# Six weight pieces converted beside the attention instead of ten, a later pipeline for each piece, nine paired slices, and routing steps moved

## The chip, the cores and the metric

The kernel runs on one core of a Trainium2 chip. The metric is the device time of one execution in microseconds (us), as the median of several runs. On the core five engines work side by side, each through its own list of instructions in order: PE (TensorE, the matmuls; its weight loads are shown apart), DVE (VectorE), ACT (ScalarE), POOL (GpSimd) and SP (SyncE), which here issues the transfers of the DMA engines. The order on each engine is the order in which the program's lines run; an instruction that waits holds up all that stand behind it on its engine.

## What is computed

Three layers follow one another, for 4 sequences of 576 positions (2304 tokens) and a model width of 512.

```python
scores = scale * np.matmul(q, k.transpose(0, 1, 3, 2))        # 4 batches, 8 heads of 64
Dmat = np.where(rel >= 0, gamma ** rel, 0.0)                  # a decay for each head, no softmax
attn = np.matmul(scores * Dmat, v)
...
x = attn rearranged to (2304, 512)
h = ((x @ w_a) * (x @ w_b)) @ w_out                           # 512 -> 1536 -> 512
...
logits = h @ w_gate + modality_bias[modality_id]              # 8 experts
e_idx = np.argmax(logits, axis=1)
gate_w = softmax(logits)[e_idx]
out[mask] = gate_w * (np.maximum(h[mask] @ w1[e], 0) @ w2[e]) # for each expert e: 512 -> 1024 -> 512
```

The three weights of the middle layer (`w_a`, `w_b`, `w_out`) come as float64, read as pairs of 32-bit words, and are turned into float32 on the chip. Nearly all products are made from a high and a low part (`xh`, `xl`; `w[:, 0]`, `w[:, 1]`), three matmuls for each.

## The kernel before

**Attention.** A loop over `i` from -1 to 20 (L476) handles 20 chunks of up to 128 rows, five for each sequence (64, 128, 128, 128, 128 rows). In iteration `i` the program issues the loads of chunk i+4 on SP, scales chunk i+1 on POOL (`a_scale`), makes its scores on PE (`sc`, L358), multiplies the scores of chunk i by the mask on DVE (`rt`, L371), and lets PE make the output of chunk i from the carried state (`o`, L409), the new state (`S`, L390) and the output from `rt` (`o`, L422). Three chunks of 384 tokens stay on the core or are written to `xsp` and fetched again later (`a_spill`, L465; `load_x`, L1020; `split_x`, L1022 to L1025, a cast on ACT and a subtraction on POOL).

**Weight pieces.** The dense layer's weights are 12 slices `fc` of three pieces each (columns of `w_a`, columns of `w_b`, rows of `w_out`), 36 pieces in the order of use. The class `Conv` takes each piece through stages, one for each call of `cv.step`: a load of 512 KB by SP (L250), ACT's Abs (L259), four DVE operations (L262, L266, L270, L274), and at the end ACT's cast (L281) with a DVE subtraction (L282) behind it. `cv.step(new)` first advances the pieces that are under way and then loads `new` more. Ten pieces pass through it beside the attention, the rest in the hooks of the dense layer, as many for each step as `CV_MOE` says.

**Dense layer.** It has 72 steps, one for each chunk of 384 tokens and each slice. A step is `gemm1` (24 matmuls into two PSUM banks `ab`, L597; then `a` on ACT, `g` on DVE L605, `gh` on ACT, `gl` on DVE L609), the step's hooks, and then `gemm2` of the step before (9 matmuls into three banks `acc`, L617). The first two token chunks (n = 1 and 2) take the slices alternately up to slice `PAIR`, so that a weight slice is needed only every second step; after these, chunk 1 does the rest of its slices and then chunk 2 (steps up to 23). From step 24 on there are 12 steps for each of the other four chunks.

**Routing.** When a chunk has its last step, its three tiles of 128 tokens are routed in parts that `route_parts` makes: part 0 and part 1 are four dot products each on DVE (`scr`, L534), part 2 is the choice of the expert on DVE (ending in `ohb`, L556), part 3 two small matmuls on PE (`rk`, L565 and L566) and the token's place behind them. A table says in which of the following hooks each part (tile, part) stands: `halves` for the first chunk, `one_each` for the next, `spread` for the last one, whose parts fall into the first two slots of the expert layer. The entry 0 is put directly behind the chunk's last `gemm2`.

**Experts.** Slots of 384 tokens of one expert follow (`slot`, L918; matmuls L881 and L898), each with loads and splits of the next slot's weights and the gather of its tokens as hooks.

Of the kernel before, what the change touches and what calls it, by code (L numbers as in the profile page):

```python
# [99 lines left out]
def build(  # L100
# [17 lines left out]
    ctx.enter_context(  # L118
        tc.manual_schedule(engines={ET.PE, ET.DVE, ET.Activation, ET.SP, ET.Pool})
    )  # L120
    CV_ATT = 10
    CV_AT = (2, 3, 4, 6, 7, 8, 11, 12, 13, 16)
    SPILL = 0
    CV_MOE = (2, 1, 2, 1, 2, 2, 1, 2, 2, 2, 2, 1, 2, 2, 2, 0)
    PAIR = 8
    WARM = (6, 4)

    cp = ctx.enter_context(tc.tile_pool(name="cp", bufs=1))
# [24 lines left out]
    def unit(name, shape, dt=F32):  # L153
        return up.tile(shape, dt, name=name, tag="u")
# [74 lines left out]
    class Conv:  # L229
# [23 lines left out]
        def advance(self, c):  # L253
            c["n"] += 1
            i, raw = c["i"], c["raw"]
            fc, j = divmod(i, 3)
            if c["n"] == 2:
                t = c["t"] = unit(f"cv{i}", [P, 512], U32)
                nc.scalar.activation(out=t.bitcast(F32), in_=raw[:, :, 1].bitcast(F32), func=AF.Abs)  # L259
            elif c["n"] == 3:  # L260
                t = c["t"]
                nc.vector.tensor_scalar(  # L262
                    out=t.bitcast(F32), in0=t.bitcast(F32), scalar1=k1, scalar2=k2,
                    op0=ALU.max, op1=ALU.min,
                )
                nc.vector.tensor_scalar(  # L266
                    out=t, in0=t, scalar1=3, scalar2=0x3FFFFFFF,
                    op0=ALU.logical_shift_left, op1=ALU.bitwise_and,
                )
                nc.vector.scalar_tensor_tensor(  # L270
                    out=t, in0=raw[:, :, 0], scalar=29, in1=t,
                    op0=ALU.logical_shift_right, op1=ALU.bitwise_or,
                )
                nc.vector.scalar_tensor_tensor(  # L274
                    out=t, in0=raw[:, :, 1], scalar=0xC0000000, in1=t,
                    op0=ALU.bitwise_and, op1=ALU.bitwise_or,
                )
            elif c["n"] == 4:
                t = c["t"]
                w = wts[fc][j] = unit(f"w{fc}_{j}", [P, 2, 512], F32R)  # L280
                nc.scalar.copy(w[:, 0, :], t.bitcast(F32))  # L281
                nc.vector.tensor_sub(w[:, 1, :], t.bitcast(F32), w[:, 0, :].bitcast(F32))  # L282
                self.live.remove(c)
# [12 lines left out]
    chunks = [(b, c) for b in BATCHES for c in range(5)]  # L296
    n_ch = len(chunks)
# [131 lines left out]
    def a_spans(i):  # L429
        b, c, n, r0 = geo(i)  # L430
        t0 = r0
        while t0 < r0 + n:
            ch = t0 // NT
            m = min(r0 + n, (ch + 1) * NT) - t0
            yield ch, t0 - r0, t0 % NT, m
            t0 += m
# [9 lines left out]
    def a_lo(i):  # L446
        for ch, a, d, m in a_spans(i):
            if ch in ORDER[:2]:
                xh, xl = xt[ch]
                for hf in range(2):  # L450
                    k = slice(NP // 2 * hf, NP // 2 * (hf + 1))
                    nc.vector.tensor_sub(
                        xl[:, k, d : d + m], A[i]["o"][hf][:, :, a : a + m],
                        xh[:, k, d : d + m].bitcast(F32),
                    )
            elif d + m == NT:
                spill.append((i + SPILL, ch))
        A[i].clear() if chunks[i][1] == 4 else None
# [9 lines left out]
    cv = Conv()  # L468
# [7 lines left out]
    for i in range(-1, n_ch + 1):  # L476
        if 3 <= i + 4 < n_ch:
            a_load(i + 4)
        if i + 1 < len(WARM):
            warm(WARM[i + 1])  # L480


        if i == -1:
            a_turn(0)
            a_turn(1)
        if 0 <= i + 1 < n_ch:
            a_scale(i + 1)
            a_scores(i + 1)
        if 0 <= i < n_ch:
            a_mask(i)  # L490
        if i >= 1:
            a_lo(i - 1)
            a_spill(i - 1)
        if i >= 0 and chunks[min(i, n_ch - 1)][1] > 0:
            cv.step(1 if cv.loaded < CV_ATT and i in CV_AT else 0)
        if 1 <= i and i + 2 < n_ch:
            a_turn(i + 2)
        if 0 <= i < n_ch:
            a_inter(i)
            a_state(i)  # L500
            a_blocks(i + 1)
            a_intra(i)
            a_hi(i)
        if i == 0:
            a_turn(2)
# [516 lines left out]
    def split_x(at, k):  # L1022
# [2 lines left out]
        nc.gpsimd.tensor_sub(xl[:, k, :], xl[:, k, :].bitcast(F32), xh[:, k, :].bitcast(F32))  # L1025

    halves = {
        0: [(0, 0)],
        1: [(0, 1), (1, 0)],
        2: [(1, 1)],  # L1030
        3: [(2, 0), (2, 1)],
        5: [(0, 2)],
        6: [(0, 3), (1, 2)],
        8: [(1, 3), (2, 2)],
        10: [(2, 3)],
    }
    one_each = {i: [divmod(i, 4)] for i in range(12)}
    quick = {
# [14 lines left out]
        6: [(2, 0)],  # L1053
        8: [(1, 3), (2, 1)],
        9: [(2, 2)],
        10: [(2, 3)],
    }


    steps = [(n, fc) for fc in range(PAIR) for n in ORDER[:2]]  # L1060
    steps += [(n, fc) for n in ORDER[:2] for fc in range(PAIR, NFA)]
    steps += [(n, fc) for n in ORDER[2:] for fc in range(NFA)]
# [3 lines left out]
    for i in range(2 * NFA):  # L1066
        hooks[i].append(lambda i=i: cv.step(CV_MOE[min(i, len(CV_MOE) - 1)]))
    hooks[1].append(setup)
# [160 lines left out]
```

## Time and profile before

| | before |
|---|---|
| median of 3 runs | 781.68 us (781.29 to 782.35) |
| the profiled execution's own time | 781.75 us |
| its span, first to last instruction | 779.9 us |
| mean granted TensorE clock | 0.989 |
| busy share PE / weight loads / DVE / ACT / POOL | 97% / 88% / 61% / 34% / 20% |
| attention, first slice's `gemm1` of the dense layer begins at | 85.1 us |

All rows below are from the profiled execution; their times count from the start of its span, which lies 1.85 us (781.75 less 779.9) inside its own time. A busy PE is not a PE at its full rate, so busy shares tell where another engine was the limit only when they are read for a stretch.

### The profile page before, as it was taken

The numbers are of one execution on the slowest core, as the hardware profiler recorded it, in microseconds if no ns is written. First come the engines' busy times: TensorE is split into PE (matmuls) and PEld (weight loads), VectorE is DVE, ScalarE is ACT, GpSimd is POOL, SyncE is SP. The second block draws the span as 40 slices with busy tenths as digits, with TensorE's granted clock in tenths as the row PEclk, the third lists the DMA queues.
The fourth block names the chain that finished last, engine by engine and source line by source line (L and its number), as shares of the span: only waits on it lengthen the run. The fifth ranks groups of instructions, "written<-read, shape, count | busy, mean of one in ns | idle before, by whom it ended". The sixth has DMA issues, their size and how long they took to land.

```text
span 779.9 us, 12645 instructions
## 1 busy us (share of the span) xinstructions
PE 753.1 (97%) x4818; PEld 684.4 (88%) x4818; DVE 472.7 (61%) x1222; ACT 264.5 (34%) x519; POOL 154.1 (20%) x181
## 2 busy tenths in 40 slices
PE   7979999999899999999999999999999999999994
PEld 4867899998799899999999999999998899999993
DVE  1699658888768565444554456766887744445520
ACT  2546334444222211221122112125443525353611
POOL 6656000000011310110021000123215233140302
PEclk9999999999999999999999999999999999999998
DMA  9997702231412000200020001042845485465201
GB/s 298 346 373 285 274 9 101 82 108 54 136 54 82 1 1 1 82 1 0 1 82 1 1 0 41 1 146 113 315 161 81 158 286 173 128 199 176 82 1 46
DMA packets 29446, 87.31 MB, mean 112 GB/s; under 512 B 6591, under 2 KB 6751, under 8 KB 29376
## 3 DMA queue, kind: packets, MB, share of 16 engines
q1 hardware_dynamic: 25040, 76.49, 29.3%
q0 software_dynamic: 4336, 9.92, 4.1%
q8 instruction: 40, 0.66, 0.4%
q14 instruction: 30, 0.25, 0.1%
HBM read 73.64 MB, written 13.01 MB: 111 GB/s over the span
## 4 chain that ended last, share of the span: by engine, by line
PE 72%; DVE 15%; DMA 7%; issue 3%; ACT 2%; SPq 0%; POOLq 0%; DVEq 0%; ACTq 0%; POOL 0%
PE ab L597 30%; PE acc L617 15%; PE h L881 11%; PE y L898 10%; DMA idt<-perm,gidx 6%; DVE scr L534 3%; DVE cv L270 2%; DVE w L282 2%; DVE cv L266 2%; PE sc L358 1%; PE o L422 1%; DVE gl L609 1%; DVE g L605 1%; DVE cv L262 1%; ACT gh L607 1%
## 5 line engine op out<-in xcount | busy, mean ns | idle before, releaser
L597 PE MATMUL ab<-xh,w 128*128 128x384 f32 x1152 | 275.9, 336 | 2.9 <-ACT w L281 1.9
L597 PEld LDWEIGHTS ab<-xh,w 128*128 128x128 f32 x1152 | 208.7, 188 | 9.4 <-ACT w L281 2.2
L597 PE MATMUL ab<-xl,w 128*128 128x384 f32 x576 | 163.0, 337 | 0.0
L617 PE MATMUL acc<-w,gh 128*128 128x512 f32 x432 | 113.5, 398 | 0.0
L605 DVE TENSOR_TENSOR g<-ab,a 128x384 f32<-128x384 f32 x72 | 40.0, 556 | 120.1 <-ACT a L603 97.1
L534 DVE SCALAR_TENSOR_TENSOR scr<-row,wg 128x512 f32<-128x512 f32 x144 | 104.7, 729 | 4.6 <-ACT row L521 0.5
L597 PEld LDWEIGHTS ab<-xl,w 128*128 128x128 f32 x576 | 105.7, 188 | 1.0
L603 ACT COPY a<-ab 128x384 f32<-128x384 f32 x72 | 34.4, 478 | 187.8 <-PE ab L597 187.8
L617 PEld LDWEIGHTS acc<-w,gh 128*128 128x128 f32 x432 | 79.5, 189 | 12.7
L607 ACT CAST gh<-g 128x384 fp32r<-128x384 f32 x72 | 36.9, 513 | 114.5 <-DVE g L605 114.5
L815 DVE TENSOR_TENSOR el<-er,eh 128x1024 fp32r<-128x1024 f32 x56 | 67.8, 1222 | 12.5 <-ACT eh L814 12.5
L609 DVE TENSOR_TENSOR gl<-g,gh 128x384 fp32r<-128x384 f32 x72 | 40.2, 558 | 41.7 <-ACT gh L607 41.7
L888 DVE SCALAR_TENSOR_TENSOR hl<-h,hh 128x384 fp32r<-128x384 f32 x48 | 26.7, 555 | 63.8 <-ACT hh L886 59.0
L881 PE MATMUL h<-sh,el 128*128 128x384 f32 x192 | 64.7, 337 | 0.0
L881 PE MATMUL h<-sh,eh 128*128 128x384 f32 x192 | 64.7, 337 | 0.0
L881 PE MATMUL h<-sl,eh 128*128 128x384 f32 x192 | 64.5, 336 | 0.0
L617 PE MATMUL acc<-w,gl 128*128 128x512 f32 x216 | 61.3, 392 | 0.0
L1025 POOL TENSOR_TENSOR xl<-xl,xh 128x384 fp32r<-128x384 f32 x16 | 19.9, 1265 | 196.2 <-ACT xh L1024 177.3
L814 ACT CAST eh<-er 128x1024 fp32r<-128x1024 f32 x56 | 57.5, 1042 | 2.2 <-DMA er<-in_w1r_dram 2.2
L577 POOL DMA_INDIRECT perm<-tg,ix x18 | 18.8, 1046 | 195.8 <-DVE ix L575 170.3
L886 ACT ACTIVATE hh<-h 128x384 fp32r<-128x384 f32 x48 | 23.6, 492 | 95.9 <-PE h L881 87.2
L617 PEld LDWEIGHTS acc<-w,gl 128*128 128x128 f32 x216 | 40.6, 188 | 9.3
(165 smaller groups left out, 1003.0 us busy)
## 6 DMA issues: line engine op xcount, KB each, us to landing
er<-in_w1r_dram SPq DMA_DIRECT2D x28, 512.0 KB, 4.7
er<-in_w2r_dram SPq DMA_DIRECT2D x28, 512.0 KB, 5.0
raw<-in_wab_dram SPq DMA_DIRECT2D x24, 512.0 KB, 6.6
kv<-in_kv_dram SPq DMA_DIRECT2D x16, 512.0 KB, 8.2
raw<-in_wout_dram SPq DMA_DIRECT2D x12, 512.0 KB, 5.8
x2d<-row SPq DMA_DIRECT2D x18, 256.0 KB, 2.3
qk<-in_qf_dram SPq DMA_DIRECT2D x16, 256.0 KB, 8.1
xsp<-xf SPq DMA_DIRECT2D x4, 768.0 KB, 5.0
```

The lines of the kernel that those rows point to most:

```text
L534: nc.vector.scalar_tensor_tensor(out=scr, in0=row, scalar=1.0, in1=wg[e // 2][:, e % 2, :], op0=ALU.mult, op1=ALU.mult, accum_out=R["l"][: ...
L597: nc.tensor.matmul(ps[j], lhsT=ws[j][:, wi, k, :], rhs=x[:, k, :], start=(k == 0 and q == 0), stop=(k == KC - 1 and q == 2),)
L603: nc.scalar.copy(a, ps[0])
L605: nc.vector.tensor_mul(g, ps[1], a)
L607: nc.scalar.copy(gh, g)
L609: nc.vector.tensor_sub(gl, g, gh.bitcast(F32))
L617: nc.tensor.matmul(accs[t], lhsT=x[:, t * P : (t + 1) * P], rhs=w[:, wi, :], start=(fc == 0 and q == 0), stop=(fc == NFA - 1 and q == 2),)
L814: nc.scalar.copy(hi, raw)
L815: nc.vector.tensor_sub(lo, raw, hi.bitcast(F32))
L881: nc.tensor.matmul(ps, lhsT=w[:, fc % 2, k, :], rhs=x[:, k, :], start=(k == 0 and q == 0), stop=(k == KC - 1 and q == 2),)
L888: nc.vector.scalar_tensor_tensor(out=hl, in0=ps, scalar=0.0, in1=hh.bitcast(F32), op0=ALU.max, op1=ALU.subtract)
L898: nc.tensor.matmul(y, lhsT=x[:, t * P : (t + 1) * P], rhs=w, start=(fc == 0 and q == 0), stop=(fc == NFF - 1 and q == 2),)
```

## The change

In `Conv` each stage comes one call of `cv.step` later: the Abs in the third call instead of the second, the four DVE operations in the fourth, the cast and the subtraction in the fifth. `cv.step` stands before `a_lo` and `a_spill` in the attention loop, and it runs in every iteration from 1 on, where it had left out the first chunk of each sequence. The numbers of pieces loaded change: 12 loads stand in the attention, six of them so late that these pieces are still under way when the dense layer begins, and 24 in the dense layer instead of 26. `PAIR` is 9 instead of 8, so that chunk 1 has its last step at 20 instead of 19, and chunk 2 at 23 as before; the loads and `split_x` of the third chunk come one hook later with it. The table `halves` is written anew, and in `spread` the last tile's last part stands one hook later. The counts of instructions on the engines are the same; line numbers in the changed kernel are one or two lower.

```diff
-    CV_ATT = 10
-    CV_AT = (2, 3, 4, 6, 7, 8, 11, 12, 13, 16)
+    CV_ATT = {2: 1, 4: 1, 6: 1, 9: 1, 11: 1, 14: 1, 17: 2, 18: 1, 19: 2, 20: 1}
-    CV_MOE = (2, 1, 2, 1, 2, 2, 1, 2, 2, 2, 2, 1, 2, 2, 2, 0)
-    PAIR = 8
+    CV_MOE = (2, 2, 1, 2, 1, 2, 2, 1, 2, 1, 2, 2, 1, 2, 1, 0)
+    PAIR = 9
...
-            if c["n"] == 2:
+            if c["n"] == 3:
...
-            elif c["n"] == 3:
+            elif c["n"] == 4:
...
-            elif c["n"] == 4:
+            elif c["n"] == 5:
...
         if i >= 1:
+            cv.step(CV_ATT.get(i, 0))
             a_lo(i - 1)
             a_spill(i - 1)
-        if i >= 0 and chunks[min(i, n_ch - 1)][1] > 0:
-            cv.step(1 if cv.loaded < CV_ATT and i in CV_AT else 0)
...
     halves = {
-        0: [(0, 0)],
-        1: [(0, 1), (1, 0)],
-        2: [(1, 1)],
-        3: [(2, 0), (2, 1)],
-        5: [(0, 2)],
-        6: [(0, 3), (1, 2)],
-        8: [(1, 3), (2, 2)],
-        10: [(2, 3)],
+        0: [(0, 0), (0, 1)],
+        1: [(1, 0), (1, 1)],
+        2: [(2, 0), (2, 1)],
+        3: [(0, 2)],
+        4: [(0, 3), (1, 2)],
+        5: [(1, 3)],
+        6: [(2, 2)],
+        8: [(2, 3)],
     }
...
     spread = {
-        10: [(2, 3)],
+        11: [(2, 3)],
```

The first place is DVE in the attention, from the mask product of chunk 9 to that of chunk 11 (`rt9` to `rt11`; `cv3` and `w0_2` are pieces of weights). Before:

```order
L371 TENSOR_TENSOR rt9_691<-sc9_0_616,mask_89 128x512
L371 TENSOR_TENSOR rt9_691<-sc9_1_617,mask_89 128x512
L282 TENSOR_TENSOR w0_2_694<-cv2_570,w0_2_694 128x512
L262 TENSOR_SCALAR cv3_636<-cv3_636 128x512
L266 TENSOR_SCALAR cv3_636<-cv3_636 128x512
L270 SCALAR_TENSOR_TENSOR cv3_636<-raw3_505,cv3_636 128x512
L274 SCALAR_TENSOR_TENSOR cv3_636<-raw3_505,cv3_636 128x512
L371 TENSOR_TENSOR rt10_746<-sc10_0_681,mask_89 64x4x64
L371 TENSOR_TENSOR rt10_746<-sc10_1_682,mask_89 64x4x64
L371 TENSOR_TENSOR rt11_796<-sc11_0_736,mask_89 128x512
```

The same place on DVE in the changed kernel:

```order
L370 TENSOR_TENSOR rt9_674<-sc9_0_606,mask_89 128x512
L370 TENSOR_TENSOR rt9_674<-sc9_1_607,mask_89 128x512
L281 TENSOR_TENSOR w0_1_677<-cv1_561,w0_1_677 128x512
L370 TENSOR_TENSOR rt10_727<-sc10_0_664,mask_89 64x4x64
L370 TENSOR_TENSOR rt10_727<-sc10_1_665,mask_89 64x4x64
L261 TENSOR_SCALAR cv2_680<-cv2_680 128x512
L265 TENSOR_SCALAR cv2_680<-cv2_680 128x512
L269 SCALAR_TENSOR_TENSOR cv2_680<-raw2_501,cv2_680 128x512
L273 SCALAR_TENSOR_TENSOR cv2_680<-raw2_501,cv2_680 128x512
L370 TENSOR_TENSOR rt11_781<-sc11_0_717,mask_89 128x512
```

Before, a subtraction and the four operations of the next piece stood together between two mask products, and none in the next gap; now one of the two kinds stands in each gap, and the piece is one behind.

The second place is DVE after step 20 of the dense layer, where chunk 1 (tiles 3, 4 and 5) is routed while chunk 2 does its last slices (`g2_9` is chunk 2, slice 9; a row with x2 is two dot products). Before:

```order
L609 TENSOR_TENSOR gl2_8_2506<-g2_8_2502,gh2_8_2504 128x384
L534 SCALAR_TENSOR_TENSOR scr3_0_2527,l3_2526<-row3_2517,wg0_2411 128x512 x2
L534 SCALAR_TENSOR_TENSOR scr3_0_2527,l3_2526<-row3_2517,wg1_2413 128x512 x2
L605 TENSOR_TENSOR g2_9_2560<-ab2_9_1_2533,a2_9_2546 128x384
L609 TENSOR_TENSOR gl2_9_2564<-g2_9_2560,gh2_9_2562 128x384
L534 SCALAR_TENSOR_TENSOR scr3_4_2566,l3_2526<-row3_2517,wg2_2415 128x512 x2
L534 SCALAR_TENSOR_TENSOR scr3_4_2566,l3_2526<-row3_2517,wg3_2417 128x512 x2
L534 SCALAR_TENSOR_TENSOR scr4_0_2572,l4_2571<-row4_2520,wg0_2411 128x512 x2
L534 SCALAR_TENSOR_TENSOR scr4_0_2572,l4_2571<-row4_2520,wg1_2413 128x512 x2
L605 TENSOR_TENSOR g2_10_2618<-ab2_10_1_2591,a2_10_2604 128x384
```

DVE in the changed kernel, from the same chunk's last step (now slice 9 of chunk 2 stands ahead of the first dots):

```order
L607 TENSOR_TENSOR gl2_9_2549<-g2_9_2545,gh2_9_2547 128x384
L532 SCALAR_TENSOR_TENSOR scr3_0_2570,l3_2569<-row3_2560,wg0_2454 128x512 x2
L532 SCALAR_TENSOR_TENSOR scr3_0_2570,l3_2569<-row3_2560,wg1_2456 128x512 x2
L532 SCALAR_TENSOR_TENSOR scr3_4_2575,l3_2569<-row3_2560,wg2_2458 128x512 x2
L532 SCALAR_TENSOR_TENSOR scr3_4_2575,l3_2569<-row3_2560,wg3_2460 128x512 x2
L603 TENSOR_TENSOR g2_10_2608<-ab2_10_1_2581,a2_10_2594 128x384
L607 TENSOR_TENSOR gl2_10_2612<-g2_10_2608,gh2_10_2610 128x384
L532 SCALAR_TENSOR_TENSOR scr4_0_2615,l4_2614<-row4_2563,wg0_2454 128x512 x2
L532 SCALAR_TENSOR_TENSOR scr4_0_2615,l4_2614<-row4_2563,wg1_2456 128x512 x2
L532 SCALAR_TENSOR_TENSOR scr4_4_2620,l4_2614<-row4_2563,wg2_2458 128x512 x2
L532 SCALAR_TENSOR_TENSOR scr4_4_2620,l4_2614<-row4_2563,wg3_2460 128x512 x2
L603 TENSOR_TENSOR g2_11_2666<-ab2_11_1_2639,a2_11_2652 128x384
```

The 24 dots of the three tiles stood between the steps 20 to 24, as 4, 8, 4 and 8; now they start one step later and stand as 8, 8 and 8 in front of the same end. After them DVE has the choice for tile 3 behind step 24 (before: behind step 25), and the choice for tile 4 behind step 25 (before: 27).

The third place is PE, where the place of tile 4 is asked for (`rk4`). Before, it stood behind `gemm1` of step 28 (`ab0_4`) and ahead of `gemm2` of step 27:

```order
L597 MATMUL ab0_4_1_2975<-xh0_2471,w4_1_1670 128x384
L565 LDWEIGHTS tri_94
L565 MATMUL rk4_3018<-ohb4_2901,tri_94 128x8
L566 LDWEIGHTS ones_95
L566 MATMUL rk4_3018<-ohb4_2901,ones_95 128x8
L617 MATMUL acc0_0_2814<-w3_2_1552,gh0_3_2946 128x512
```

PE in the changed kernel at the same instruction:

```order
L595 MATMUL ab0_2_1_2856<-xh0_2514,w2_1_1361 128x384
L563 LDWEIGHTS tri_94
L563 MATMUL rk4_2907<-ohb4_2837,tri_94 128x8
L564 LDWEIGHTS ones_95
L564 MATMUL rk4_2907<-ohb4_2837,ones_95 128x8
L615 MATMUL acc0_0_2843<-w1_2_1224,gh0_1_2801 128x512
```

The two small matmuls stand behind `gemm1` of step 26 now (`ab0_2`), two steps earlier on PE, and `gemm2` of step 25 stands behind them.

## Rows read from the trace of the kernel before

**Rows 1.** The page, part 1: busy time, share of the span and instructions.

```profile
PE 753.1 (97%) x4818; PEld 684.4 (88%) x4818; DVE 472.7 (61%) x1222; ACT 264.5 (34%) x519; POOL 154.1 (20%) x181
```

**Rows 2.** Busy time in attention's second part: span, PE, PEld, DVE, ACT, POOL, clock, DMA.

```profile
34.80:85.10 50.30, 44.84 (x784) 36.96 (x781) 47.27 (x79) 28.33 (x67) 25.36 (x27) 0.97 0.90 322
```

**Rows 3.** Chain of waits, 20 to 86 us: start, length, engine and tile.

```profile
22.16 1.09 PE sc L358 x16
...
25.57 0.61 PE sc L358 x16
...
28.39 1.09 PE sc L358 x16
...
31.15 1.09 PE sc L358 x16
...
34.04 0.90 PE o L422 x16
```

**Rows 4.** Timeline of PE in the attention: start, length, instruction [idle before, releaser].

```profile
51.59 0.89 PE L422 MATMUL o<-rt,kv 64*64 64x64 f32 x16 [2.90 <-DVE rt L371]
```

**Rows 5.** Groups of DVE instructions, 34.8 to 85.1 us: busy us, mean ns, idle before.

```profile
L282 DVE TENSOR_TENSOR w<-cv,w 128x512 fp32r<-128x512 f32 x9 | 8.0, 894 | 2.0 <-ACT w L281 2.0
```

**Rows 6.** Chain of waits, 0 to 330 us, in the paired steps.

```profile
102.06 4.18 PE ab L597 x24
...
108.33 4.18 PE ab L597 x24
...
147.24 1.25 DVE w L282 x2
...
159.12 1.26 DVE w L282 x2
...
166.48 1.26 DVE w L282 x2
```

**Rows 7.** Timeline of PE in the paired steps and behind them.

```profile
133.23 0.33 PE L597 MATMUL ab<-xh,w 128*128 128x384 f32 x1
...
207.81 0.44 PE L597 MATMUL ab<-xh,w 128*128 128x384 f32 x1 [1.86 <-ACT w L281]
...
218.22 1.55 PE L617 MATMUL acc<-w,gh 128*128 128x512 f32 x6
```

**Rows 8.** Busy time behind that wait, columns as in rows 2.

```profile
208.00:212.00 4.00, 3.89 (x14) 3.47 (x14) 1.34 (x3) 0.65 (x2) 0.00 (x0) 0.64 0.84 267
```

**Rows 9.** Timeline of DVE while chunk 1 is routed.

```profile
220.66 0.69 DVE L534 SCALAR_TENSOR_TENSOR scr<-row,wg 128x512 f32<-128x512 f32 x1 [0.47 <-ACT row L521]
...
226.37 0.69 DVE L534 SCALAR_TENSOR_TENSOR scr<-row,wg 128x512 f32<-128x512 f32 x1
...
233.37 0.55 DVE L605 TENSOR_TENSOR g<-ab,a 128x384 f32<-128x384 f32 x1
...
239.17 0.55 DVE L605 TENSOR_TENSOR g<-ab,a 128x384 f32<-128x384 f32 x1
...
240.78 0.69 DVE L534 SCALAR_TENSOR_TENSOR scr<-row,wg 128x512 f32<-128x512 f32 x1
...
246.40 0.55 DVE L605 TENSOR_TENSOR g<-ab,a 128x384 f32<-128x384 f32 x1
...
259.22 0.16 DVE L541 TENSOR_TENSOR l<-l,mb 128x8 f32<-128x8 f32 x1
...
261.21 0.16 DVE L541 TENSOR_TENSOR l<-l,mb 128x8 f32<-128x8 f32 x1
```

**Rows 10.** Timeline of POOL in the same stretch.

```profile
226.35 3.00 POOL L1025 TENSOR_TENSOR xl<-xl,xh 128x384 fp32r<-128x384 f32 x2 [140.69 <-ACT xh L1024]
```

**Rows 11.** Timeline of PE, first place of chunk 1.

```profile
256.62 0.18 PE L565 MATMUL rk<-ohb,tri 128*128 128x8 bf16 x1 [0.64 <-DVE ohb L556]
```

**Rows 12.** Timelines of PE and of DVE, last chunk's routing in slot 1.

```profile
591.43 0.17 PE L565 MATMUL rk<-ohb,tri 128*128 128x8 bf16 x1 [1.62 <-DVE ohb L556]
...
598.31 0.17 DVE L832 CAST iid<-idt 128x3 uint32<-128x3 f32 x1 [3.67 <-DMA idt<-perm,gidx]
```

## The prediction

> **What bounds the kernel now.** The page comes first: PE is busy over 97% of the span [rows 1], so a gain can only lie in the few places where PE waits or runs slower than it could, and a loss wherever the change makes it wait anew. The second view is the busy time by stretch. From 34.8 us to the end of the attention PE has 44.84 us of 50.30, but DVE has 47.27 [rows 2]: there DVE is the fuller engine, by more than the whole span shows. The third view is the chain of waits, since it tells whether PE's own work would have ended earlier. Where it runs from PE to PE, the starts of the scores give the length of an iteration that only PE limits [rows 3]: 3.41 us (22.16 to 25.57), 2.82, 2.76, and a regular one of 3.79 (31.15 to 34.04, and .90 for the `o` that ends it). Behind that the chain leaves PE, and PE's timeline shows why: at 51.59 it had stood 2.90 us for a mask product `rt` on DVE [rows 4]. The fourth place is the paired steps. There a step of PE alone is 6.27 us (102.06 to 108.33) [rows 6], and later ones are longer. The fifth is the routing behind step 20, where DVE has little room between two steps [rows 9]. In the experts PE has few waits; one of 1.62 us is touched by the change [rows 12].
>
> **A. Attention.** I count what PE alone would take for iterations 7 to 19: five regular ones at 3.79, two each at 3.41, 2.82 and 2.76, and the last two without the transposes and the scores that they no longer have, an estimate of 3.2 and 1.62 from the same rows. That is 18.95 + 6.82 + 5.64 + 5.52 + 4.82 = 41.75 us. They take 85.10 - 34.94 = 50.16, so 8.4 us are lost. Nine subtractions L282 end pieces in this stretch [rows 5]; in the changed kernel the pieces start later and apart, so six end there, and the six that are loaded from iteration 17 on reach DVE only in the dense layer. A piece costs DVE at least 2.86 us (worked out under B where POOL is still), more here, where an L282 takes 894 ns [rows 5] against 630 (1.26 for two [rows 6]). DVE's 47.27 us fall by 3 x 2.86 = 8.6 to 38.7 or less, which is below PE's 41.75. Then PE bounds the stretch. The order of DVE helps too: a gap between two mask products holds either the four operations or one subtraction, 2.2 or .63 us at the unslowed price, where it held both. The transfers were at a share of .90 [rows 2]; three loads of 512 KB fewer relieve them, and the Abs comes a call later, so that a load has an iteration more to land. I leave 1.1 us of the 8.4 for single late mask products, so **-7.3**, with bounds of -3 (if the rest waits for transfers) and -8.4 (nothing lost).
>
> **B. Paired steps.** How long DVE needs for a step is read where the chain runs through DVE [rows 6]: from 147.24 to 159.12 two steps with three pieces, 11.88 us, and from 159.12 to 166.48 one step with two pieces, 7.36. The difference is one piece more in twice the rest: a piece is 2 x 7.36 - 11.88 = 2.84 to 2.86, and the rest of a step (`g`, `gl`) 1.65. Before, 26 pieces stand in the 15 hooks from 3 to 17: 1.73 for each step, 1.65 + 1.73 x 2.86 = 6.6 us, more than PE's 6.27. DVE falls behind, and the pieces come late: at 207.81 PE has waited 1.86 us for the cast of a piece [rows 7], and in the 4 us behind it the granted clock is .64 of the full 2.4 GHz [rows 8], after PE had stood still for that wait alone. From 133.23 (step 8) to 218.22 (end of `gemm1` of step 20) are 84.99 us [rows 7], for twelve steps and one `gemm1` of 4.18: 12 x 6.27 + 4.18 = 79.42. So 5.57 us are lost here. In the changed kernel six pieces are already under way, and 30 stand in the hooks 0 to 18: 1.58 for each step, 1.65 + 1.58 x 2.86 = 6.17, under 6.27. The ninth paired slice gives the pieces of slice 9 one more step. The pieces that are in flight at the start (slices 2 and 3) end in the hooks 1 to 4, and their slices are wanted at steps 4 and 6, so two steps of 6.27 hide them; without that cover one late piece would cost its 2.86. **-5.6**, with bounds of -4 (one such piece late somewhere) and -5.6.
>
> **C. Routing of chunk 1.** Here DVE's work is put together more closely, and I follow it from the end of `gemm1` of step 21, called 0. The first dots start 2.44 later (218.22 to 220.66 [rows 7, 9]). Eight dots take 5.62 (240.78 to 246.40), from `g` to the first dot are 1.61 (239.17 to 240.78), and eight dots beside POOL's two subtractions take 7.0 (226.37 to 233.37) [rows 9, 10], since these slow some of them. So `g` of step 22 comes at 2.44 + 5.62 = 8.06 instead of 6.27, `g` of step 23 at 8.06 + 1.61 + 7.0 = 16.67 instead of 12.54. The split of the third chunk, which is one hook later with `PAIR`, stands behind these: its last two POOL subtractions end 3.0 [rows 10] behind a cast pair that follows `gh` of step 23, at about 21.2, whereas `gemm1` of step 24 wants the third part at 14.6 + 2.1 = 16.7 and the last at 17.8. PE waits some 3.2 us there, and step 24's `gemm1` ends at 22 instead of 18.8. DVE is at 25.28 by then (1.61 and 7.0 more), takes the choice for tile 3, and the four dots of the next chunk's first tile (row copy behind the choice, 28.8 to 31.6), `g` of step 25 at 31.6, four more dots, a place and a choice (together 1.99, 259.22 to 261.21 [rows 9]): `ohb` of tile 4 is there at 38.25. PE wants it behind `gemm1` of step 26, unstalled at 31.5, with `gemm2` of step 25 queued behind. So PE is 6.75 late in all. Two such waits should bring the lower clock back; 4 us at .64 cost 4 x .36 = 1.4 [rows 8]. From this comes off what the kernel before loses at the same work, .64 at 256.62 [rows 11] and about .4 of slower clock with it. The late work stops there: behind it DVE has only a choice, places and `g` for each step, against PE's 6.27. **+7.1**, with bounds of +5.5 (no slower clock) and +8.5 (twice as much).
>
> **D. The last part.** The wait of 1.62 at 591.43 goes, since the last place comes one hook later [rows 12]. But DVE waits there for the token list until 598.31, 3.67 us, and the `hl` behind it is late for PE; a hook later this may give half of it back. **-0.8**, from -1.6 to 0. The moved lines without a term of their own (`cv.step` ahead of the spill) only exchange the order of two transfers on SP, a load and a store, in stretches that A covers.
>
> The sum is made against the profiled execution, 781.75 us, which lies .07 above the median: 781.75 - 7.3 - 5.6 + 7.1 - 0.8 = **775.2**.
>
> **The rivals.** *The routing loss is small* (0.12): if PE's third part of the split comes from the POOL subtractions in time, because ACT's casts slip in between the dots sooner than I let them, the 3.2 us of PE's wait go and the second wait stays; C is about +3, and the time 771. Against it: ACT's cast stands behind `gh`, and that behind a `g` that follows eight dots. *The gains are smaller* (0.13): with A at its lower bound, the time is 779.5; for it speaks the transfers' share of .90 in [rows 2], against it that PE's wait in [rows 4] was for DVE. *Nothing changes* (0.08): the busiest engine bounds the kernel, and its instructions are the same; then the time stays at 781.7. By [rows 1] that engine is PE. The Trainium skill says this in Perfetto Trace Analysis, section Identifying the Most-Contended Engine: the engine with the highest occupancy is the one to optimise first, and for TensorE the weight loads' share is the better measure. Here this share is 88%, still the highest beside PE's own. For the stretch of [rows 2] the order is the reverse, 36.96 us of weight loads under DVE's 47.27, and the page itself grants, in Optimization Strategy, that the engine can change by regime. *Slower* (0.06): the mechanism is the routing with its waits in full. If transfers and not DVE set the attention, A is 0, and C at its upper bound of 8.5 more than outweighs B and D: 781.75 - 5.6 + 8.5 - 0.8 = 783.9. It decides when A yields less than about .7 with C at that bound; three pieces less on DVE speak against it.
>
> **How the numbers follow.** The forecast's own case (773 to 778) has 0.61, and the predicted time is its sum. The range of 770.5 to 779.8 takes in most of the case of the small routing loss and most of that of the smaller gains; it leaves out the unchanged and the slower case. Less than 0.2% is 1.56 us, about what a measurement can tell from no change: faster is below 780.1, slower above 783.2. Faster holds the forecast's case, the small routing loss and all but .02 of the smaller gains, 0.84; that .02 is shared by the same, 0.09, and slower, 0.07.
>
> **What would show it.** A is right if the first `gemm1` of the dense layer begins at about 78 instead of 85.1, and DVE has less busy time than PE from iteration 7 on; it is wrong if PE still waits for `rt`, or waits for a tile that a transfer brings. B is right if the twelve steps from 8 to 20 take 75.2 to 76 us without a wait for a weight. C is right if PE waits for `xl` in step 24's `gemm1` and then for `ohb` of tile 4 behind step 26, about 3.2 and 3.5 us; if PE runs through there, the kernel is faster than forecast by up to 7. D is right if PE's wait in slot 1 is gone and none above .8 takes its place. The prediction is wrong as a whole if C's waits do not come, or if A's stretch stays above 46 us.

## The result and the profile after

The changed kernel takes 775.43 us (median of 4 runs, 774.52 to 776.74) against 782.01 in the runs beside it; the ratio is 0.9918, with an interval of 0.9901 to 0.9935. The profiled execution has 775.61 us and a span of 773.7. It is 0.8% faster, and the time is .2 us from the forecast.

The page's first part answers to [rows 1]: the shares are the same as before, though 6 us are gone.

```profile
PE 750.8 (97%) x4818; PEld 683.0 (88%) x4818; DVE 471.5 (61%) x1222; ACT 264.2 (34%) x519; POOL 152.3 (20%) x181
```

So the time has to be compared by stretch. Five starts on PE bound the stretches that the prediction speaks of: the scores at the beginning of iteration 7 (L357, before L358), the first `gemm1` of the dense layer, and the `gemm1` of steps 8, 20 and 34 (the steps from there to step 69 take 220.78 us in every run). These are the rows of PE's timeline for the kernel before:

```profile
34.85 0.71 PE L358 MATMUL sc<-qk 64*128 64x128 f32 x8
...
85.09 0.45 PE L597 MATMUL ab<-xh,w 128*128 128x384 f32 x1
...
214.03 0.34 PE L597 MATMUL ab<-xh,w 128*128 128x384 f32 x1
...
303.27 0.51 PE L597 MATMUL ab<-xh,w 128*128 128x384 f32 x2
```

And for the changed kernel, with step 8 at 126.58, which is at 133.23 in [rows 7]:

```profile
35.79 0.94 PE L357 MATMUL sc<-qk 64*128 64x128 f32 x12
...
78.47 0.44 PE L595 MATMUL ab<-xh,w 128*128 128x384 f32 x1
...
126.58 0.33 PE L595 MATMUL ab<-xh,w 128*128 128x384 f32 x1
...
201.78 0.33 PE L595 MATMUL ab<-xh,w 128*128 128x384 f32 x1
...
298.29 0.51 PE L595 MATMUL ab<-xh,w 128*128 128x384 f32 x2
```

The differences of such rows, in us, for all profiled kernels of this study (the last part is from step 69 to the end of PE's last product). The stretches come from one execution each, the median time from several; where an edit leaves a stretch alone, its column shows how far executions of one program differ.

| kernel | attention from iteration 7 | steps 8 to 20 | steps 20 to 34 | last part | median time |
|---|---|---|---|---|---|
| before | 50.24 | 80.80 | 89.24 | 245.13 | 782.01 |
| changed | 42.68 | 75.20 | 96.51 | 244.06 | 775.43 |
| late choice | 42.53 | 75.20 | 92.83 | 245.53 | 773.08 |
| split in one hook | 42.49 | 75.20 | 95.11 | 243.90 | 775.04 |
| both | 46.58 | 75.20 | 92.73 | 244.27 | 774.39 |
| spread back | 42.95 | 75.20 | 94.95 | 245.33 | 776.33 |
| more DVE work | 59.52 | 75.20 | 96.53 | 245.22 | 790.12 |
| more loads | 47.14 | 75.20 | 96.52 | 245.32 | 779.43 |
| stages back | 44.36 | 75.20 | 94.96 | 243.99 | 777.51 |
| eight slices, loads earlier | 42.45 | 77.34 | 89.24 | 245.20 | 770.59 |
| xl first | 43.30 | 75.20 | 96.55 | 245.18 | 776.45 |
| before, less DVE work | 46.04 | 79.24 | 89.22 | | |
| before, fewer loads | 54.01 | 79.25 | 89.26 | 245.11 | 784.38 |
| eight slices, evenly, xl first | 43.45 | 76.98 | 89.26 | 243.92 | 769.61 |

The change gives 7.56 us in the attention and 5.60 in the paired steps, takes 7.27 behind them, and gives 1.07 at the end. Iteration 7 begins .94 us later than before; in the kernels with the same program up to there it begins anywhere from 34.6 to 36.4, so this is not the change. The balance is .94 - 7.56 - 5.60 + 7.27 - 1.07 = -6.0, against 6.2 between the spans.

In the attention PE is now the fuller engine. The busy time by stretch, with the columns of [rows 2]:

```profile
34.80:81.00 46.20, 45.66 (x818) 38.64 (x813) 39.74 (x67) 27.08 (x66) 25.68 (x27) 1.00 1.01 370
```

PE has 45.66 of 46.20 us, DVE 39.74. The window ends 2.5 us into the dense layer; up to 78.5 us DVE has 38.34 of 43.70 us, where it had 47.27 of 50.30. Of the waits that [rows 4] stood for, one is left in PE's timeline, and it is not for `rt`:

```profile
66.14 1.16 PE L357 MATMUL sc<-qk 64*128 64x128 f32 x14 [0.54 <-DVE xl L451]
```

Before, PE waited 5.45 us for `rt` in this stretch, in four places (1.25, 2.90, .79 and .51), and behind the longest wait it ran at the lower of its two clock levels for a time (the column behind POOL's is the granted clock; .50 is 1.2 of 2.4 GHz):

```profile
52.00:56.00 4.00, 4.00 (x46) 3.22 (x44) 3.50 (x7) 2.05 (x5) 0.52 (x1) 0.57 0.98 301
```

An estimate of what that costs is PE's busy time times what the granted clock lacks to 1.00: 4 x .43 = 1.7 us. So of the 7.56 us some 4.9 are waits and 1.7 the clock.

Behind the paired steps PE waits in two places. The same view, with the granted clock behind the second one from the busy times by stretch:

```profile
230.46 0.62 PE L595 MATMUL ab<-xh,w 128*128 128x384 f32 x2 [1.35 <-ACT xh L1022]
...
232.09 0.62 PE L595 MATMUL ab<-xl,w 128*128 128x384 f32 x2 [1.01 <-POOL xl L1023]
...
250.21 0.18 PE L563 MATMUL rk<-ohb,tri 128*128 128x8 bf16 x1 [3.04 <-DVE ohb L554]
```

```profile
252.00:256.00 4.00, 4.00 (x17) 3.63 (x16) 2.34 (x17) 1.38 (x5) 1.31 (x3) 0.68 0.00 0
```

So the third chunk's split comes late for step 24, and then `ohb` of tile 4 late behind step 26. DVE's timeline shows the cause; these are the `g` of steps 22 to 25 and that `ohb`, and they answer to [rows 9]:

```profile
220.30 0.55 DVE L603 TENSOR_TENSOR g<-ab,a 128x384 f32<-128x384 f32 x1
...
228.90 0.55 DVE L603 TENSOR_TENSOR g<-ab,a 128x384 f32<-128x384 f32 x1
...
237.48 0.55 DVE L603 TENSOR_TENSOR g<-ab,a 128x384 f32<-128x384 f32 x1
...
243.53 0.55 DVE L603 TENSOR_TENSOR g<-ab,a 128x384 f32<-128x384 f32 x1
...
249.85 0.30 DVE L554 CAST ohb<-oh 128x8 bf16<-128x8 f32 x1
```

`gemm1` of step 21 ends at 212.2 by PE's timeline, so these are 8.1, 16.7, 25.3, 31.3 and 37.7 behind it. The prediction's list was 8.06, 16.67, 25.28, 31.6 and 38.25.

### The profile page after: what moved, and what is told of

Same layout as the page of the kernel before. It is cut to its first block, busy times and chain, and to the rows that moved or that the text cites. A ratio compares the mean times of both kernels' runs of the same rounds, so it can differ in the third digit from the quotient of the medians.

```text
span 773.7 us, 12643 instructions
## 1 busy us (share of the span) xinstructions
PE 750.8 (97%) x4818; PEld 683.0 (88%) x4818; DVE 471.5 (61%) x1222; ACT 264.2 (34%) x519; POOL 152.3 (20%) x181
```

## The experiments

My theory: DVE bounded the attention (A) and the paired steps (B), and the ninth paired slice presses the routing of chunk 1 together, so that DVE bounds there (C). The rivals are told with each run.

### Where the loss behind step 20 comes from

**Late choice.** Choices and places of chunk 1 back at the steps where they stood.

```diff
-        3: [(0, 2)],
-        4: [(0, 3), (1, 2)],
-        5: [(1, 3)],
-        6: [(2, 2)],
-        8: [(2, 3)],
+        4: [(0, 2)],
+        5: [(0, 3), (1, 2)],
+        7: [(1, 3), (2, 2)],
+        9: [(2, 3)],
```

> The changed kernel, with the choices and places of chunk 1 put back to the steps 25 to 30 where they stood before the change; its dots stay at 8, 8 and 8. If PE's second wait (3.04 us for ohb of tile 4 and 1.4 us of lower clock behind it) comes from the choices standing too early behind a late DVE, it goes and only the first wait (for the split of the third chunk, 3.3 us in step 24) is left: 771 us. The rival, that the dots alone have put DVE behind and PE waits at the same place for gl instead, gives 775.

Measured: 773.08 us (ratio 0.9891, 0.9859 to 0.9922). The last part explains 1.5 us of what is missing to 771, and the lower clock another 1.0: it comes behind the first wait here, so that step 24 takes 10.61 us instead of 9.56, at a granted clock of .84. Steps 20 to 34 take 92.83, 3.7 less than in the changed kernel. PE waits at the split alone:

```profile
230.88 0.62 PE L595 MATMUL ab<-xh,w 128*128 128x384 f32 x2 [1.34 <-ACT xh L1022]
...
232.51 1.01 PE L595 MATMUL ab<-xl,w 128*128 128x384 f32 x2 [1.01 <-POOL xl L1023]
```

The second wait was for the choice in its early place; the rival's wait for `gl` does not come.

**Split in one hook.** All four parts of the third chunk's split in step 22.

```diff
-                hooks[i + 2 + k // 2].append(lambda at=at, k=k: split_x(at, k))
+                hooks[i + 2 + (k // 2 if at > 2 else 0)].append(lambda at=at, k=k: split_x(at, k))
```

> The changed kernel, with all four parts of the third chunk's split in the hook of step 22 instead of two in step 22 and two in step 23. If both of PE's waits have one cause, DVE's row of 24 dots, the first wait goes (step 24 takes 6.3 instead of 9.6 us) and the second grows by the same 3 us, since DVE is no earlier: 775 us. The rival, that each wait has a cause and a price of its own, gives 772.

Measured: 775.04 us (0.9921, 0.9899 to 0.9943), as expected for one common cause. The profile shows why it is no faster: step 24 takes 6.90 instead of 9.56, and PE waits for `gh` and for two `ohb` in its place.

```profile
230.35 1.65 PE L615 MATMUL acc<-w,gh 128*128 128x512 f32 x6 [0.37 <-ACT gh L605]
...
239.38 0.17 PE L563 MATMUL rk<-ohb,tri 128*128 128x8 bf16 x1 [2.51 <-DVE ohb L554]
...
249.17 0.18 PE L563 MATMUL rk<-ohb,tri 128*128 128x8 bf16 x1 [1.65 <-DVE ohb L554]
```

The last of these waits ends 48.6 us behind the start of step 20 (200.6 to 249.17), and in the changed kernel 48.4 (201.78 to 250.21): what the first wait gave up came back whole, since DVE has `ohb` of tile 4 no earlier. The 1.4 us between 95.11 and 96.51 are another thing, the lower clock that the changed kernel has behind its last wait and this execution does not have there (granted 1.00 from 252 to 256 us; it has it in step 25, at .84, where PE waits for `ohb` afterwards in any case). It comes and goes in one program. The run with `spread` back, told below, differs from the changed kernel only in the last part, waits as long at the same place, and keeps the full clock:

```profile
250.22 0.18 PE L563 MATMUL rk<-ohb,tri 128*128 128x8 bf16 x1 [3.06 <-DVE ohb L554]
```

```profile
252.00:256.00 4.00, 4.00 (x24) 3.92 (x23) 2.34 (x17) 1.38 (x5) 1.31 (x3) 1.00 0.00 0
```

Its steps 20 to 34 take 94.95 us. So the two waits have one cause, and 1.56 us of the changed kernel's 96.51 are the clock.

**Both edits.**

> Both of these edits together. If the two waits are what the routing costs, neither is left, steps 20 to 34 take what they took before the change or less, and the time is 768 us. The rival, that the lateness of DVE only moves on to later steps, gives 771 to 775.

Measured: 774.39 us (0.9902, 0.9877 to 0.9928), and 92.73 for the steps: no better than the late choice alone, so my expectation fell and the rival holds (the time also has a longer attention in it, see below). DVE stays behind by its 24 dots, whatever waits for it; the `ohb` is now that of tile 3:

```profile
234.29 1.64 PE L615 MATMUL acc<-w,gh 128*128 128x512 f32 x6 [0.36 <-ACT gh L605]
...
241.52 1.64 PE L615 MATMUL acc<-w,gh 128*128 128x512 f32 x6 [0.72 <-ACT gh L605]
...
250.59 0.18 PE L563 MATMUL rk<-ohb,tri 128*128 128x8 bf16 x1 [2.56 <-DVE ohb L554]
```

This run also shows how the attention can vary with an unchanged program: it takes 46.58 us, since PE waits 1.0 us longer at the place of the changed kernel's .54, and then has the lower clock for a time, which by the same estimate costs 3.2 us.

```profile
66.00 2.07 PE L357 MATMUL sc<-qk 64*128 64x128 f32 x14 [1.56 <-DVE xl L451]
```

```profile
66.00:70.00 4.00, 4.00 (x34) 3.22 (x34) 3.66 (x8) 0.90 (x2) 0.00 (x0) 0.50 1.01 401
70.00:74.00 4.00, 4.00 (x55) 3.60 (x52) 0.97 (x3) 1.70 (x4) 0.84 (x2) 0.71 1.02 415
```

The longer wait can be followed to DVE. The last piece operation ahead of `xl` takes 1.79 us here, beside a POOL operation that begins with it:

```profile
63.81 1.79 DVE L273 SCALAR_TENSOR_TENSOR cv<-raw,cv 128x512 uint32<-128x512 uint32 x1
```

```profile
63.80 1.26 POOL L341 TENSOR_TENSOR qks<-qk,qtc 128x512 f32<-128x512 f32 x1 [1.03 <-PE o L421]
```

The same operation in the changed kernel:

```profile
65.06 0.69 DVE L273 SCALAR_TENSOR_TENSOR cv<-raw,cv 128x512 uint32<-128x512 uint32 x1
```

**Eight slices, loads earlier.** The ninth paired slice and the new `halves` undone, the last loads about a hook earlier.

```diff
-    CV_MOE = (2, 2, 1, 2, 1, 2, 2, 1, 2, 1, 2, 2, 1, 2, 1, 0)
-    PAIR = 9
+    CV_MOE = (2, 2, 1, 2, 2, 2, 1, 2, 2, 1, 2, 2, 2, 1, 0)
+    PAIR = 8
...
```

> The changed kernel with eight paired slices and the routing table of before, and with the last loads of the dense layer about a hook earlier, since slices 9 to 11 are wanted a step earlier. If the ninth paired slice is what forces the dots together and costs 7.3 us, and a mean of 1.6 to 1.7 pieces for each step is what DVE can bear, the paired steps stay free of waits or lose under 2 us, and steps 20 to 34 lose about 1 us: 768 to 770 us. The rival, that the ninth slice is needed for the gain of 5.6 us in the paired steps, gives 773 to 775.

Measured: 770.59 us (0.9849, 0.9826 to 0.9872), a little above the range expected. Steps 20 to 34 take 89.24, what they took before the change, and steps 8 to 20 77.34, 2.1 more than with nine slices. So the ninth slice and its routing table together cost 7.3 us, and the slice saves 2.1; 3.5 of the 5.6 us in the paired steps come without it. Slice and table were undone at once. The late choice alone took 3.7 of the 7.3 away with the ninth slice left in; whether a table that spreads the dots over more steps would save the rest as well was not tried.

### What bounded the attention

**More DVE work, no load.** Three sets of five operations on the mask, read by nothing.

```diff
+        if i in (8, 12, 15):
+            d = tmp(f"d{i}", [P, 512])
+            m0, m1 = (mask[:, j].rearrange("p a s -> p (a s)") for j in range(2))
+            nc.vector.tensor_scalar(out=d, in0=m0, scalar1=k1, scalar2=k2, op0=ALU.max, op1=ALU.min)
+            nc.vector.tensor_scalar(out=d, in0=m1, scalar1=k1, scalar2=k2, op0=ALU.max, op1=ALU.min)
+            for _ in range(3):
+                nc.vector.tensor_sub(d, m0, m1)
```

> The changed kernel with three more sets of five DVE operations of 128x512 in the attention (iterations 8, 12 and 15, on the mask, with results that nothing reads), about the work of three pieces, and no load with them. If DVE's work bounded the attention before, the dense layer's first gemm1 comes several us later again (between 3 and 8, DVE is then at 48 us of busy time against 41.75 of PE), and the time is 779 to 783 us. The rival, that the loads set it, gives 775.4 and no change of that start.

Measured: 790.12 us (1.0087, 1.0053 to 1.0121), above the range expected. The attention takes 59.52 us, 16.8 more, far over the 8.6 us of three pieces. The work stands ahead of single mask products: the first set keeps DVE for 7.5 us (41.84 to 49.38), and PE waits 10.0 us in four places. Behind the first and the last of them PE runs at a granted clock of .50 for some 9.5 and 5.5 us, which costs 7.5 us by the estimate above. So the direction is shown, but much of the size is the clock.

```profile
50.11 1.97 PE L421 MATMUL o<-rt,kv 128*64 128x128 f32 x16 [5.87 <-DVE rt L370]
```

```profile
50.00:54.00 4.00, 3.89 (x32) 3.36 (x32) 3.90 (x9) 0.74 (x2) 0.00 (x0) 0.50 0.18 74
```

**Before, less DVE work.** The same question from the other side, in the kernel before.

```diff
+            elif c["n"] == 3 and i in (3, 4, 5, 6):
+                pass
             elif c["n"] == 3:
```

> The kernel before, with the four DVE operations of the pieces 3 to 6 left out (their weights are then other numbers) and all its loads as they were: 8.8 us or more of DVE less. If DVE bounded the attention, it takes 43 to 45 us from iteration 7 on instead of 50.2 and the time is 775 to 777 us. The rival, that the transfers did, gives 50 and 782.

Its whole time (934.92 us) tells nothing, since the experts' slots depend on the numbers. The attention takes 46.04 us instead of 50.24, with all the loads as they were. In its first 26.50 us DVE falls from 24.03 us of busy time to 20.66 and PE rises from 22.35 to 24.45, while the transfers' share is full in both (1.02 and 1.00). The direction is the theory's, the size (4.2) short of the 5 to 7 expected: PE waits 2.76 us where it waited 5.45, and the other 1.5 are about the lower clock of before, which this execution does not have. First the kernel before, then this run:

```profile
34.80:61.30 26.50, 22.35 (x379) 18.41 (x376) 24.03 (x35) 14.16 (x33) 13.34 (x11) 0.94 1.02 376
```

```profile
34.80:61.30 26.50, 24.45 (x456) 20.22 (x454) 20.66 (x29) 16.14 (x38) 13.55 (x11) 1.00 1.00 354
```

**Before, fewer loads.** Three loads left out, DVE's work kept.

```diff
+            if i in (3, 4, 5):
+                self.live.append({"i": i, "raw": self.raw2, "n": 0})
+                return
             raw = unit(f"raw{i}", [P, 512, 2], U32)
+            if i == 2:
+                self.raw2 = raw
```

> The kernel before, with the loads of the pieces 3, 4 and 5 left out (their stages work on the data of piece 2) and all its DVE work as it was: three transfers of 512 KB less. If transfers bounded the attention, at 1.27 us for each, it takes 46.4 us from iteration 7 on instead of 50.2 and the time is 778. If DVE bounded it, it takes 49 to 50 and the time is 781 to 782.

Measured: 784.38 us (1.0032, 1.0015 to 1.0049), with an attention of 54.01 us: longer, not shorter, while the transfers' share from 34.8 to 61.3 us falls to .74 (1.02 in the kernel before). None of the ten runs is under 782.07 us, where the rival asked for 778, so transfers did not set the attention before. PE waits 8.0 us here, and the lower clock costs some 3.3 by the estimate (5.45 and 1.7 before). Where part of it comes from is seen on DVE and POOL. One DVE operation of .69 us takes 3.80, as long as three POOL operations in a row; ACT's cast of a piece comes late behind it, and PE waits 2.67 us for that:

```profile
38.28 3.80 DVE L275 SCALAR_TENSOR_TENSOR cv<-raw,cv 128x512 uint32<-128x512 uint32 x1
```

```profile
38.27 1.04 POOL L349 TENSOR_TENSOR qks<-kv,ca 64x512 f32<-64x512 f32 x1 [3.78 <-DMA kv<-in_kv_dram]
39.27 1.26 POOL L347 TENSOR_TENSOR qks<-qk,qtc 128x512 f32<-128x512 f32 x1
40.49 1.03 POOL L349 TENSOR_TENSOR qks<-kv,ca 128x512 f32<-128x512 f32 x1
```

The Trainium skill says in SBUF — State Buffer, section Who interferes with whom, that a DVE instruction with two inputs in SBUF and a POOL instruction that reads SBUF exclude one another, and that the one that issues first holds the other up. The trace agrees with these rows, and here the wait lasted over three POOL instructions. It is the only operation so long in the attentions of the fourteen profiles; the next longest takes 1.79 us.

**More loads, no DVE work.** In the changed kernel.

```diff
             cv.step(CV_ATT.get(i, 0))
+            if i in (3, 7, 8):
+                for j in range(2):
+                    d = tmp(f"d{i}_{j}", [P, 512], U32)
+                    nc.sync.dma_start(out=d, in_=wab.bitcast(U32)[11, :, j, 0:512])
```

> The changed kernel with three more loads of 512 KB in the attention (iterations 3, 7 and 8, where the kernel before had its own; nothing reads them), and no DVE work with them. If DVE was the bound, the dense layer's first gemm1 moves by less than 1 us and the time is 775 to 776.5 us. The rival, that the transfers set the attention, gives 1.27 us for each of the loads, 3.8 in all: 779 us.

Measured: 779.43 us (0.9948, 0.9922 to 0.9973; ten runs from 775.7 to 781.8). This speaks for the rival in the changed kernel, where the share of the transfers is 1.01. PE does not wait for a transfer, though: it waits for `xl` at the same place as above, 1.84 us, and then has the lower clock (.59 and .55 from 66 to 74 us). Of the 4.5 us that the attention is longer, 1.3 are the wait and some 3 the clock.

```profile
67.46 2.07 PE L357 MATMUL sc<-qk 64*128 64x128 f32 x14 [1.84 <-DVE xl L451]
```

Since the run with both routing edits had the same wait and clock without these loads, this run does not settle how much the loads themselves cost; that they bring the longer attention more often is likely, not shown.

**Stages back.** Each stage of a piece one call earlier again.

```diff
-            if c["n"] == 3:
+            if c["n"] == 2:
...
-            elif c["n"] == 4:
+            elif c["n"] == 3:
...
-            elif c["n"] == 5:
+            elif c["n"] == 4:
```

> The changed kernel with each stage of a piece one call earlier, as before the change. If the number of pieces is what counts and the later stages only hide the landing of a load, the attention is longer by less than 1 us: 775 to 776.5 us. The rival, that the later stages are what removes the late mask products, gives a start of the dense layer 3 us or more later, 778.5 us and above.

Measured: 777.51 us (0.9937, 0.9916 to 0.9959), between the two. The attention is 1.7 us longer, with a wait of .30 for `rt` again and 1.55 for `xl`, and steps 0 to 8 lose .7. A wait of 1.56 for `xl` also stands in the run with both routing edits, whose stages are the late ones, so the 1.7 us lie within what executions of one program differ by. What the later stages give in the attention is not shown beyond the .30; most of its gain is there without them.

**xl first.** `a_lo` ahead of `cv.step`, as before the change.

```diff
-            cv.step(CV_ATT.get(i, 0))
             a_lo(i - 1)
+            cv.step(CV_ATT.get(i, 0))
```

> The changed kernel with the subtractions that make xl put back ahead of the pieces' stages in an iteration; the load of a piece still stands ahead of the spill. If PE's wait of .5 to 1.8 us for xl in iteration 16, and the lower clock that follows it in some executions, come from DVE's piece work standing ahead of xl, the wait goes, the attention takes 42 us from iteration 7 on, and the time is 773.5 to 775. The rival, that DVE is late there whatever its order, gives a wait for rt in its place and 775.4.

Measured: 776.45 us (0.9925, 0.9900 to 0.9949). The wait for `xl` is gone and one of .84 us for ACT's cast of a piece stands there; the attention takes 43.30, and the time is above the 773.5 to 775 expected. The rival holds in the time, though the wait is not for `rt`, as it had it.

```profile
66.73 1.16 PE L408 MATMUL o<-qks,sbd 64*64 64x128 f32 x16 [0.84 <-ACT w L280]
```

### The last part, and the best version

**Spread back.**

```diff
-        11: [(2, 3)],
+        10: [(2, 3)],
```

> The changed kernel with the last tile's last part back one hook earlier in slot 1. If the gain at the end comes from that part, PE's wait of about 1.6 us for ohb returns and the time is 776.5 us. The rival, that the end became shorter for another reason, gives 775.4 and no wait.

Measured: 776.33 us (0.9933, 0.9908 to 0.9959). The wait is there again:

```profile
584.86 0.17 PE L563 MATMUL rk<-ohb,tri 128*128 128x8 bf16 x1 [1.62 <-DVE ohb L554]
```

Yet the last part above has two values with the new place, about 244 and about 245.3 (five profiles each), and only the second with the old one (three profiles). The five near 244 have DVE's wait for the token list at 3.2 to 3.5 us, the other five at 4.4 to 4.8. In the late-choice run it is 4.80 (3.31 in the profile of the changed kernel), and PE waits twice for work behind it:

```profile
590.40 0.17 DVE L830 CAST iid<-idt 128x3 uint32<-128x3 f32 x1 [4.80 <-DMA idt<-perm,gidx]
```

```profile
592.30 0.96 PE L896 MATMUL y<-eh,hl 128*128 128x512 f32 x3 [0.84 <-DVE sm L558]
...
609.37 0.96 PE L896 MATMUL y<-eh,hl 128*128 128x512 f32 x3 [0.87 <-DVE hl L886]
```

So the step gives about 1.2 us when the list lands early and nothing when it lands late. By the median times alone its worth is not shown: the intervals of this run and of the changed kernel overlap.

**Eight slices, evenly, xl first.** The run with eight slices, its hooks spread anew, and `a_lo` ahead of `cv.step`.

```diff
-    CV_MOE = (2, 2, 1, 2, 2, 2, 1, 2, 2, 1, 2, 2, 2, 1, 0)
+    CV_MOE = (2, 2, 1, 2, 2, 1, 2, 2, 1, 2, 2, 1, 2, 2, 0)
...
```

> The changed kernel with eight paired slices and the routing table of before, the pieces of the dense layer spread more evenly over the hooks (2, 2, 1 repeated, none behind hook 13), and xl ahead of the pieces' stages. If the pieces of the run with eight slices were late only where three hooks of two pieces stood together, the 2.1 us that it lost in the steps 8 to 20 shrink to under 1, and the attention loses no more than in the run with xl first: 767.5 to 769.5 us. The rival, that 1.67 pieces for each step are simply more than DVE can bear, leaves the 2 us in these steps: 770 to 771.

Measured: 769.61 us (0.9852, 0.9821 to 0.9884). It and the run before it with eight slices are the fastest, about 12 us under the kernel before and, by the medians, 5 to 6 under the changed one. The steps 8 to 20 run free of waits but for one, in step 19, where a piece of the last slice is late; that step takes 8.04 us, 1.77 more than the others. So the loss did not shrink to the under 1 us that I expected; spreading the pieces moved it into one step. The rival stands: with 1.67 pieces for each step the prediction's count gives 1.65 + 1.67 x 2.86 = 6.43 us, over the 6.27 of PE.

```profile
198.16 0.45 PE L595 MATMUL ab<-xh,w 128*128 128x384 f32 x1 [1.12 <-ACT w L280]
```

## Why the prediction was right

**A, -7.3: measured -7.56.** The count of PE's own time, 41.75 us, was good to .93: the attention took 42.68, and its profile shows PE busy throughout. That DVE was the cause is shown from both sides (more DVE work +16.8 us, less -4.2, each with a change of the clock in it; fewer loads no gain). After the change the transfers are not cleared in the same way: three more loads gave 779.43 us. What I left out: `cv.step` was also moved ahead of `xl` on DVE, not only two transfers on SP; in its own run that order moved a wait and no time. It also did not name the lower clock, which was some 1.7 us of what the kernel before lost here.

**B, -5.6: measured -5.60.** The steps take 75.20 us, 12 times 6.27, in every run with nine slices. The price of a piece (2.86) and the two rates (6.6 and 6.17 a step) carried it. That the size fits so well rests on the profile before, from which it was read: 1.56 of the 5.60 us are the lower clock behind the wait of 1.86 in [rows 7]. In the runs of the kernel before with less DVE work and with fewer loads PE waits 1.87 and 1.86 us at the same place, the clock stays at 1.00, and the twelve steps take 79.24 and 79.25. That DVE was the bound rests on [rows 6] and on this count; no run changed its work alone in these steps. The ninth slice's share is 2.1 or less, as the runs with eight slices lost 2.1 and 1.8 there, the second in step 19 alone.

**C, +7.1: measured +7.27.** Both waits came where they were forecast: step 24 takes 3.29 us over 6.27, and step 26 4.43 (3.04 of waiting, the rest mostly the lower clock, which goes on into step 27). The clock was forecast at 1.4; the same program with and without it differs by 1.56 (96.51 and 94.95), and without it C is 5.7, close to the bound of 5.5 that stood for this. So "two such waits should bring the lower clock back" holds for some executions only. The price was right, but not as a sum of two waits that could be taken away one by one: with the first wait taken away its time came back in the others, and with both edits 3.5 us stay (92.73 against 89.24), because DVE is behind by its 24 dots. With eight slices and the old table, which give the dots four steps instead of three, nothing of the loss is left.

**D, -0.8: measured -1.07 in this profile,** and between -1.2 and +.4 in other executions with the same order; the upper end lies .4 above the bound of 0, in the late-choice run, where waits of .84 and .87 stand in the place of the one of 1.62.

That all four terms came out within .3 us is in part luck. It holds for these two profiles, and executions of one program differ by 4 us in the attention (42.5 to 46.6) and by 1.6 in the paired steps and behind them, as the lower clock comes or stays away. The mechanism does not hang on this, the closeness does.

Neither of the two signs that would have made the prediction wrong as a whole occurred in the changed kernel's profile; an attention of more than 46 us is in the run with both routing edits, with the same program there. The occupancy rival (no change) fails since DVE, not the fuller PE, bounded two stretches. The rival of smaller gains had some truth in that the transfers' share is full in the whole attention now (1.01), and was so before only in its first part (1.02).

## What to carry to other kernels

Take busy shares by stretch, and price a change of order on the engine that is full there: counted against a PE step without waits (6.27 us, or the iterations of [rows 3]), all three large terms came out to within .3 us in one pair of profiles, and within about 4 in others. A move that delays a last step also shortens the room of what hangs on that step: the ninth slice with its table cost 7.3 us of routing for about 2 us of supply. Look at the granted clock before a difference is put down to an edit: 1.56 us of it came and went twice in stretches that no edit had touched. When two waits have one late engine behind them, edit what that engine does and not the order of those that wait.

## What was not expected of the hardware

One DVE operation took 3.80 us instead of .69 beside three POOL operations in a row. A smaller case of it, 1.79 instead of .69, stands ahead of the longer wait in the run with both routing edits; whether all of the spread of the attention, 42.5 to 46.6 us in one program, comes from this is not shown. And a wait of PE was followed by the lower clock in some executions and not in others, at the same place and with the same length: 1.56 us, then .50 and .71 in the next 8 us, but 1.55 in the run with the stages back (at 64.78), then 1.00; 3.04 and 3.06 us behind step 26, then .68 and 1.00; 1.86 us in step 19 before, then .64, but 1.87 in the run with less DVE work, then 1.00. What tells them apart stays open.
